# A planned attention-and-mixer kernel: a longer fixed cost for exponentials in its plan, normalisation off TensorE, and the order of its work found anew

## The chip, the cores and the metric

The kernel runs on one NeuronCore of a Trainium2 chip. The metric is the time of one execution on the device, in microseconds (us). The core's engines are TensorE (PE), which multiplies matrices into the eight banks of PSUM; VectorE (DVE); ScalarE (ACT), which here evaluates exp, tanh and gelu by its tables; GpSimd (POOL); and SyncE (SP), which here only issues DMAs. Each engine has its own list of instructions, in the order in which the kernel wrote them, and waits on semaphores for the others.

## The reference

Two layers, each an attention block and then a mixer block with an MLP, over 2048 tokens of width 448, with 16 heads of 28. The weights are the same in both layers.

```python
def _A_ref(x, wqkv, wo):                     # attention
    qkv = (x @ wqkv).reshape(B, S, 3, H, Dh).transpose(2, 0, 3, 1, 4)
    q, k, v = qkv[0], qkv[1], qkv[2]
    scores = jnp.einsum("bhqd,bhkd->bhqk", q, k) * (Dh ** -0.5)
    p = _softmax(scores, axis=-1)
    o = jnp.einsum("bhqk,bhkd->bhqd", p, v)
    return o.transpose(0, 2, 1, 3).reshape(B, S, D) @ wo

def _B_ref(x, w1, w2, w3, w4):               # mixer and MLP
    h = _gelu(_layernorm(x) @ w1)
    # four quarters of h shifted by +1, -1, +2, -2 tokens -> g0..g3
    hs = jnp.concatenate([g0, g1, g2, g3], axis=-1) @ w2
    x1 = x + hs
    return x1 + _gelu(_layernorm(x1) @ w3) @ w4

x = A_x
for _ in range(2):
    x = x + _A_ref(_layernorm(x), A_wqkv, A_wo)
    x = x + _B_ref(_layernorm(x), B_w1, B_w2, B_w3, B_w4)
```

## The kernel before

**A planner writes the order.** The kernel is a set of small tasks (Python generators, `t_exp`, `t_pv`, `k_proj`, `t_mixA` and so on) that yield operations: an engine, a planned duration, what is read and written. The class `Sched` runs all tasks at once on planned clocks, one per engine, and picks at each step the operation that can start first; between those that compete it goes by a priority. The order in which it picks is the order in which each engine's instructions are written, so planned durations have no effect on the chip except through that order. Where PE would stand idle in the plan, `keep_pe_busy` puts in fillers: groups of four matmuls of the identity with no use for the result (L2160). Constants at the top of the file steer the planner: `RANK` (priorities of tasks by layer and chunk), `Q_LEAD` (how early the query projection of a chunk starts), `R_RATE` and `D_RATE` (shares of score tiles that VectorE takes, by pair of segments), `PE_NORM`, and `XPAR` (some thresholds and modes).

**Scores and exponentials.** Per layer, the queries are cut into five chunks (three of 512 and two of 256 queries), the heads into four groups of four, the keys into blocks. A segment is one chunk, one head group and a run of keys; there are 68 segments, four to a part of the order (17 parts). PE makes score tiles of 128x512 (L1411). ScalarE takes them in units of three or two banks in turn: one exponential (L1649) reads 1536 or 1024 columns of PSUM and writes bf16 into the buffer `PT`. Its planned duration stands in `t_exp`. There are 2048 score tiles.

**The share of VectorE.** Some score tiles do not go to ScalarE but through a polynomial on VectorE, a chain of five instructions: L1493 (scaled, to integer), L1520 and L1522 (two multiply-add steps), L1524 (last step, to bf16) and L1527 (puts the exponent in), with the result in the buffer `PD` or in free slots of `vaug`. The task `t_scores` picks such tiles five to nine groups of scores ahead of where ScalarE is; when it takes one for a unit's third bank, ScalarE's exponential has two tiles instead of three.

**After the scores.** PE multiplies the exponentials with the values (`t_pv`, L820, `ps<-PT,vaug`). The sums of the softmax come out as an extra row. The task `t_norm` copies the result out (L1731, or L1733 where it adds to an earlier part) and, when the segment is the last for its queries, normalises in one of two ways, chosen by `PENORM`. One goes through DMA: the row of sums is loaded into `rT`, inverted (L1746), written to `rscr` in DRAM and spread over the partitions by four more DMAs into `fb`, and POOL multiplies (L1758). The other stays on the core: small f32 matmuls bring the sums together (`ps<-e,ub`, L820), VectorE inverts (L1771), PE and VectorE spread them out again (L1774, L1776, `ps<-rT,selq`), and VectorE multiplies (L1780). The last chunk of layer 1 always takes the second way.

```python
def PENORM(L, ch, g):
    return (L == 1 and ch == len(CHUNKS[1]) - 1) or (PE_NORM[L, ch] and g == 3)
```

**Mixer and MLP.** The output projection (`t_outproj`), the mixer (`t_mixA`, `t_mixB`) and the MLP (`t_w4`) of a chunk are done while the exponentials of later chunks go on. Their projections are the lines L829. Gelu needs another table of ScalarE than exp, and each change is a table load. `MODE` says, by chunk, how the mixer's gelu is done: by tanh, which shares the table of exp (L1929 on ScalarE, with L1927 on POOL and L1928 and L1930 on VectorE), or as one wide gelu (L1911) that waits to share a table load with the gelu of the MLP (L2113). When the last exponential is through, the tail begins: the gelus of the last groups are then read directly from PSUM (L2085), and PE works off the last projections.

Of the kernel before, what the change touches and what calls it, by code (L numbers as in the profile page):

```python
# [6 lines left out]
ACT = mybir.ActivationFunctionType  # L7
# [541 lines left out]
DPRIO = 2.5  # L549
DST = [('dve', 0.6), ('dve', 0.6), ('dve', 0.34), ('dve', 0.6)]  # L550
DSEG = 1
R_RATE = {(0,): 0.142, (1,): 0, (2,): 0.185, (3,): 0, (4,): 0, (5,): 0.02, (6,): 0.218, (7,): 0.001, (8,): 0, (9,): 0.095, (10,): 0.119, (11,): 0.363, (12,): 0.116, (13,): 0.0, (14,): 0, (15,): 0.04, (16,): 0.176, (17,): 0, (18,): 0, (19,): 0.261, (20,): 0.084, (21,): 0.12, (22,): 0.211, (23,): 0.279, (24,): 0.114, (25,): 0.159, (26,): 0.143, (27,): 0.211, (28,): 0, (29,): 0.129, (30,): 0.03, (31,): 0.098, (32,): 0.024, (33,): 0.0}
RLO = 6
RHI = 9
RPRIO = 0.5
# [3 lines left out]
DLO = 5  # L559
DHI = 8  # L560
DPK = 2
RANK = {('q', 0, 1): 1.485, ('q', 0, 2): 2.903, ('q', 0, 3): 1.285, ('q', 1, 0): 1, ('q', 1, 1): 1, ('q', 1, 2): 1.695, ('q', 1, 3): 2.124, ('b', 0, 0): 2.36, ('b', 0, 1): 1.442, ('b', 0, 2): 2.1, ('b', 0, 3): 3, ('b', 0, 4): 2.2, ('b', 1, 0): 1.217, ('b', 1, 1): 2.458, ('b', 1, 2): 2.616, ('b', 1, 3): 2.98, ('b', 1, 4): 2.111, ('a', 0, 0): 2.648, ('a', 0, 1): 2.105, ('a', 0, 2): 2.607, ('a', 0, 3): 1.825, ('a', 0, 4): 1.327, ('a', 1, 0): 1.819, ('a', 1, 1): 2.318, ('a', 1, 2): 1.312, ('a', 1, 3): 1.708, ('a', 1, 4): 2.524, ('k', 0, 1): 1.651, ('k', 0, 2): 1.127, ('k', 0, 3): 1.089, ('k', 1, 0): 2.088, ('k', 1, 1): 2.41, ('k', 1, 2): 1.843, ('k', 1, 3): 2.108, ('k', 1, 4): 1.983, ('c', 0, 0): 1.937, ('c', 0, 1): 1, ('c', 0, 2): 1.716, ('c', 0, 3): 2.026, ('c', 0, 4): 2.338, ('c', 1, 0): 2.542, ('c', 1, 1): 1.267, ('c', 1, 2): 1, ('c', 1, 3): 2.438, ('c', 1, 4): 1.368, ('w', 0, 0): 1.991, ('w', 0, 1): 1.492, ('w', 0, 2): 2.1, ('w', 0, 3): 2.652, ('w', 0, 4): 2.838, ('w', 1, 0): 2.361, ('w', 1, 1): 2.963, ('w', 1, 2): 2.611, ('w', 1, 3): 2.164, ('w', 1, 4): 1.394, ('o', 0, 0): 2.395, ('o', 0, 1): 1.387, ('o', 0, 2): 1.318, ('o', 0, 3): 1.195, ('o', 0, 4): 1.084, ('o', 1, 0): 2.093, ('o', 1, 1): 1.177, ('o', 1, 2): 1.823, ('o', 1, 3): 1.568, ('o', 1, 4): 1.308, ('v', 0, 1): 2.396, ('v', 0, 2): 1.93, ('v', 0, 3): 2.669, ('v', 1, 0): 1.95, ('v', 1, 1): 2.676, ('v', 1, 2): 2.257, ('v', 1, 3): 1.399, ('v', 1, 4): 2.602, ('l', 1, 0): 1.698, ('l', 1, 1): 2.543, ('l', 1, 2): 2.299, ('l', 1, 3): 1.01, ('l', 1, 4): 1.745}
Q_LEAD = {(0, 1): 34, (0, 2): 114, (0, 3): 36, (1, 0): 57, (1, 1): 67, (1, 2): 75, (1, 3): 147}
D_RATE = {(0,): 0.041, (1,): 0, (2,): 0, (3,): 0.154, (4,): 0.266, (5,): 0.481, (6,): 0.055, (7,): 0.125, (8,): 0.155, (9,): 0.747, (10,): 0.232, (11,): 0.243, (12,): 0.14, (13,): 0, (14,): 0.372, (15,): 0.002, (16,): 0.057, (17,): 0.442, (18,): 0, (19,): 0.418, (20,): 0.453, (21,): 0, (22,): 0.343, (23,): 0.024, (24,): 0.41, (25,): 0.544, (26,): 0.546, (27,): 0, (28,): 0.445, (29,): 0, (30,): 0, (31,): 0, (32,): 0.506, (33,): 0.438}
PE_NORM = {(0, 0): False, (0, 1): False, (0, 2): True, (0, 3): False, (0, 4): True, (0, 5): False, (0, 6): False, (0, 7): False, (1, 0): True, (1, 1): False, (1, 2): True, (1, 3): True, (1, 4): False, (1, 5): False, (1, 6): True, (1, 7): True}
TANHW = {(0, 11): 1, (1, 13): 1}
Sched.AGED = 0
Sched.TARGET = 0.6
# [33 lines left out]
def build_kernel(nc, A_x, A_wqkv, A_wo, B_x, B_w1, B_w2, B_w3, B_w4, out, n_layers=2):  # L602
# [8 lines left out]
    SCALE = DH ** -0.5  # L611
# [70 lines left out]
    with st:  # L682
# [3 lines left out]
        ps = st.enter_context(nc.psum_tensor("ps", [128, 8, 512], FP32))  # L686
# [52 lines left out]
        PT = sb("PT", [128, 15, 512], BF16)  # L739
# [522 lines left out]
        def t_kv(L, c):  # L1262
# [28 lines left out]
        def t_q(L, qc):  # L1291
# [240 lines left out]
        def t_scores():  # L1532
# [40 lines left out]
            while True:  # L1573
# [60 lines left out]
        def t_exp():  # L1634
            u = -1
            while True:
                u += 1
                yield ("wait", ("st", u))
                un = units[u]
                if not un:  # L1640
                    break
                if u >= 6:
                    for (si, kb, j) in units[u - 6]:
                        yield ("wait", ("pv", si, kb))
                bk = unit_banks(u)
# [3 lines left out]
                yield op("act", 0.051 + n * w * 0.000833, lambda e, bk=bk, s0=s0, n=n, w=w: e.activation(out=PT[:, s0:s0 + n, 0:w], in_=ps[:, bk[0]:bk[0] + n, 0:w], func=ACT.Exp, scale=SCALE),  # L1649
                         reads=[("ps", b) for b in bk], writes=[("pt", s0 + k) for k in range(n)], tab="exp")  # L1650
# [612 lines left out]
```

## Time and profile before

| | |
|---|---|
| Time, median of 3 runs | 1032.74 us (1032.65 to 1034.38) |
| Profiled execution | 1035.93 us, of which the span from first to last instruction is 1034.2 us |
| Busy: PE, DVE, ACT, POOL | 986.5, 769.1, 988.8, 280.4 us |
| Granted clock of TensorE, mean | 0.993 of full |
| Exponentials (L1649) | 352 of 128x1536, 449 of 128x1024 |
| First and last exponential start | 15.7 and 982.2 us |

A busy time counts an engine's own instructions, and overlapping ones once. The profile's busy share of PE contains the fillers. A duration of a single ScalarE instruction in the groups (a mean of 1571 ns for 128x1536) contains the time in which it overlaps with the one before it; the distance between two starts is shorter. The profiled execution is one run, some 3 us longer than the median of the timed runs.

### The profile page before, as it was taken

How to read it: one execution, taken by the hardware profiler on the slowest of the kernel's cores; microseconds unless marked ns; L12 is line 12 of the kernel's file. 1: busy time of each engine (PE TensorE's matmuls, PEld its weight loads, DVE VectorE, ACT ScalarE, POOL GpSimd, SP SyncE). 2: the span in 40 equal slices, each digit the busy share in tenths (PEclk: the TensorE clock that was granted, in tenths of full speed). 3: DMA queues.
4: the chain of work that ended last, by engine and by line, in shares of the span. 5: the costliest groups of instructions: out<-in, count | busy, mean ns of one | idle time of the engine just before them, and what ended most of it. 6: DMA issues, size and time to landing. Idle time of an engine off the chain costs nothing.

```text
span 1034.2 us, 35199 instructions
## 1 busy us (share of the span) xinstructions
PE 986.5 (95%) x15802; PEld 408.2 (39%) x15805; DVE 769.1 (74%) x1502; ACT 988.8 (96%) x907; POOL 280.4 (27%) x403
## 2 busy tenths in 40 slices
PE   8999999998999999999999999999999999899998
PEld 4333344333333344334434333333334434444465
DVE  8577887899888775667767976797886875776452
ACT  7999999999999999999999999998999999999952
POOL 2232223333205014431335021121543120422120
PEclk9999999999999999999999999998999999999999
DMA  4423645111105004111123033413201020120000
GB/s 120 133 69 87 145 118 148 40 28 36 35 12 116 13 11 111 43 43 24 46 79 63 32 88 112 140 46 107 64 23 38 18 68 2 41 71 15 12 15 31
DMA packets 97259, 63.25 MB, mean 61 GB/s; under 512 B 69908, under 2 KB 86372, under 8 KB 97108
## 3 DMA queue, kind: packets, MB, share of 16 engines
q1 hardware_dynamic: 93732, 52.91, 20.0%
q0 software_dynamic: 3376, 8.09, 3.0%
q8 instruction: 124, 2.03, 0.8%
q14 instruction: 27, 0.22, 0.1%
HBM read 27.12 MB, written 16.73 MB: 42 GB/s over the span
## 4 chain that ended last, share of the span: by engine, by line
ACT 80%; PE 15%; DVE 4%; issue 1%; DMA 0%; SPq 0%; DVEq 0%
ACT PT L1649 72%; PE ps L829 9%; PE ps L1411 3%; ACT h2T L2113 3%; PE ps L820 3%; ACT fb L1929 1%; DVE PD L1524 1%; ACT L1649 1%; ACT hT L1911 0%; PE ps L2160 0%; ACT L2113 0%; DVE fb L1520 0%; ACT L1911 0%; DVE PD L1527 0%; DMA PT<-in_A_wqkv_dram 0%
## 5 line engine op out<-in xcount | busy, mean ns | idle before, releaser
L1649 ACT ACTIVATE PT<-ps 128x1024 bf16<-128x1024 f32 (+1 forms) x801 | 893.5, 1328 | 9.9 <-PE ps L1411 9.5
L1411 PE MATMUL ps<-qT,kT 32*128 32x512 bf16 (+1 forms) x2560 | 315.4, 342 | 25.5 <-ACT PT L1649 18.5
L820 PE MATMUL ps<-PT,vaug 128*32 128x512 bf16 (+1 forms) x2452 | 247.0, 343 | 0.7 <-DVE ub L1733 0.6
L1411 PEld LDWEIGHTS ps<-qT,kT 32*128 32x128 bf16 x2560 | 80.7, 91 | 302.8 <-ACT PT L1649 284.5
L829 PE MATMUL ps<-xT,w 128*32 128x512 bf16 (+3 forms) x2368 | 158.7, 340 | 2.1 <-DVE hT L1898 1.7
L820 PEld LDWEIGHTS ps<-PT,vaug 128*32 128x32 bf16 x2452 | 74.8, 95 | 87.8 <-issue 71.9
L2160 PE MATMUL ps<-ident 128*32 128x256 bf16 x2188 | 102.2, 280 | 1.6 <-POOL ident L914 1.5
L829 PE MATMUL ps<-w,h2T 128*32 128x448 bf16 x1288 | 91.3, 355 | 4.1 <-ACT h2T L2113 4.1
L829 PEld LDWEIGHTS ps<-xT,w 128*32 128x32 bf16 x2368 | 63.5, 95 | 48.2 <-issue 22.9
L2089 DVE CAST h2T<-ps 128x384 bf16<-128x384 f32 (+1 forms) x84 | 52.1, 620 | 27.0 <-PE ps L829 26.0
L2160 PEld LDWEIGHTS ps<-ident 128*32 128x32 bf16 x2188 | 62.6, 98 | 21.8 <-issue 9.0
L1758 POOL TENSOR_TENSOR otn<-ub,fb 128x512 bf16<-128x512 f32 (+1 forms) x31 | 34.9, 1125 | 130.3 <-DMA fb<-rscr 130.2
L1493 DVE TENSOR_SCALAR yd<-ps 128x512 int32<-128x512 f32 x73 | 50.1, 687 | 25.3 <-PE ps L1411 24.4
L1163 POOL TENSOR_TENSOR sq<-qT 128x512 bf16<-128x512 bf16 x28 | 31.7, 1135 | 115.4 <-DVE qT L1212 111.8
L1163 POOL TENSOR_TENSOR sq<-kT 128x512 bf16<-128x512 bf16 (+2 forms) x32 | 31.6, 991 | 84.2 <-DVE kT L1177 68.8
L1522 DVE SCALAR_TENSOR_TENSOR fb<-fb,yd 128x512 f32<-128x512 f32 x68 | 51.2, 757 | 0.6
L1527 DVE SCALAR_TENSOR_TENSOR PD<-yd,PD 128x512 int16<-128x512 int16 x70 | 49.5, 709 | 1.0
L1520 DVE SCALAR_TENSOR_TENSOR fb<-yd 128x512 f32<-128x512 uint16 x68 | 47.1, 699 | 0.4
L829 PEld LDWEIGHTS ps<-w,h2T 128*32 128x32 bf16 x1288 | 34.3, 96 | 32.9 <-issue 14.3
L829 PE MATMUL ps<-xT,wq_pad 128*32 128x512 bf16 x512 | 43.3, 383 | 1.8 <-DVE vaug L1493 0.9
L1837 POOL TENSOR_SCALAR mst<-mv 128x1 f32<-128x1 f32 x32 | 7.8, 242 | 135.0 <-DVE mv L1016 133.5
L829 PE MATMUL ps<-xT,wk_pad 128*32 128x512 bf16 (+2 forms) x512 | 42.2, 363 | 0.3 <-DVE h2T L2089 0.2
(200 smaller groups left out, 1339.3 us busy)
## 6 DMA issues: line engine op xcount, KB each, us to landing
uscr<-ub SPq DMA_DIRECT2D x28, 256.0 KB, 2.0
ub<-uscr SPq DMA_DIRECT2D x28, 256.0 KB, 3.6
fb<-rscr SPq DMA_DIRECT2D x84, 64.0 KB, 2.1
xnd<-xn SPq DMA_DIRECT2D x28, 128.0 KB, 2.9
x_res<-in_A_x_dram POOLq DMA_DIRECT2D x16, 224.0 KB, 3.7
xd<-x_res SPq DMA_DIRECT2D x16, 224.0 KB, 2.4
x_res<-xd SPq DMA_DIRECT2D x16, 224.0 KB, 3.0
out_dram<-obf SPq DMA_DIRECT2D x16, 112.0 KB, 1.9
```

What stands on the lines that cost most here:

```text
L820: return lambda e: e.matmul(out=out, lhsT=lhsT, rhs=rhs, start=start, stop=stop, **kw)
L829: r.append(e.matmul(out=out[c:c + w, :], lhsT=lhsT[:, c:c + w], rhs=rhs, start=start, stop=stop, tile_position=(0, c)))
L1163: return both("sq", 0.15 + NW * 0.0018, 0.07 + NW * 0.00104, lambda e: e.tensor_tensor(out=sq[:, si, 0:NW], in0=src, in1=src, op=ALU.mult) ...
L1411: yield op("pe", (0.005 + NW * 0.00042) / nc_, lambda e, i=i, kc=kc, j=j, g=g, a=a, NW=NW, bank=bank: e.matmul(out=ps[:, bank, i * NW:(i + ...
L1493: yield op("dve", c_ps(512), lambda e: e.tensor_scalar(out=y, in0=ps[:, bi(bank), :], scalar1=SCALE * L2E * FS, scalar2=-126.0 * FS, op0=A ...
L1520: yield op(D_[0][0], D_[0][1], lambda e: e.scalar_tensor_tensor(out=q, in0=lo, scalar=E2 / E3 * FS, in1=lo, op0=ALU.add, op1=ALU.mult), re ...
L1522: yield op(D_[1][0], D_[1][1], lambda e: e.scalar_tensor_tensor(out=q, in0=q, scalar=E1 / E3 * FS * FS, in1=lo, op0=ALU.add, op1=ALU.mult) ...
L1527: yield op(D_[3][0], D_[3][1], lambda e: e.scalar_tensor_tensor(out=pdt.bitcast(I16), in0=hi, scalar=128.0, in1=pdt.bitcast(I16), op0=ALU. ...
L1649: yield op("act", 0.051 + n * w * 0.000833, lambda e, bk=bk, s0=s0, n=n, w=w: e.activation(out=PT[:, s0:s0 + n, 0:w], in_=ps[:, bk[0]:bk[0 ...
L1758: yield both("otn", 0.2 + NW * 0.0021, 0.07 + NW * 0.00104, lambda e: e.tensor_tensor(out=otn[:, g, 0:NW], in0=u, in1=rb[:, 0:NW], op=ALU. ...
L2089: ev = op("dve", c_ps(m * NW), lambda e, hr=hr, pv=pv: e.tensor_copy(out=hr, in_=pv), reads=[("ps", bi(b))], writes=hk, touch=[b])
L2160: return [e.matmul(out=ps[32 * c:32 * c + 32, bi(b), 0:256].rearrange("p (a n) -> p a n", n=128), lhsT=xn[:, 0, D:D + 32] if live else ide ...
```

## The change

The planned duration of an exponential has 0.0635 instead of 0.051 as its fixed part. The constants of the planner are replaced: `RANK`, `Q_LEAD`, `R_RATE`, `D_RATE`, some of `XPAR`, and `PE_NORM`, which is now false for every chunk but the last one of layer 1 (entries for chunks 5 to 7 have no chunk). In `XPAR`, the entry of the mixer of layer 0, chunk 1 goes from 1 to 0, that is from the wide gelu to tanh; the other entries `mg` that differ choose nothing, since chunk 0 and the last chunk of layer 1 are decided otherwise. All the rest is the planner's answer to these numbers.

```diff
...
-R_RATE = {(0,): 0.142, (1,): 0, (2,): 0.185, (3,): 0, (4,): 0, (5,): 0.02, (6,): 0.218, (7,): 0.001, (8,): 0, (9,): 0.095, (10,): 0.119, (11,): 0.363, (12,): 0.116, (13,): 0.0, (14,): 0, (15,): 0.04, (16,): 0.176, (17,): 0, (18,): 0, (19,): 0.261, (20,): 0.084, (21,): 0.12, (22,): 0.211, (23,): 0.279, (24,): 0.114, (25,): 0.159, (26,): 0.143, (27,): 0.211, (28,): 0, (29,): 0.129, (30,): 0.03, (31,): 0.098, (32,): 0.024, (33,): 0.0}
+R_RATE = {(0,): 0, (1,): 0.172, (2,): 0.006, (3,): 0.003, (4,): 0.021, (5,): 0, (6,): 0.317, (7,): 0, (8,): 0.118, (9,): 0.112, (10,): 0.118, (11,): 0.453, (12,): 0.316, (13,): 0, (14,): 0, (15,): 0.344, (16,): 0.26, (17,): 0, (18,): 0, (19,): 0.017, (20,): 0.197, (21,): 0.08, (22,): 0, (23,): 0.396, (24,): 0.016, (25,): 0, (26,): 0.013, (27,): 0.22, (28,): 0, (29,): 0.17, (30,): 0.146, (31,): 0.157, (32,): 0.079, (33,): 0.151}
...
-Q_LEAD = {(0, 1): 34, (0, 2): 114, (0, 3): 36, (1, 0): 57, (1, 1): 67, (1, 2): 75, (1, 3): 147}
-D_RATE = {(0,): 0.041, (1,): 0, (2,): 0, (3,): 0.154, (4,): 0.266, (5,): 0.481, (6,): 0.055, (7,): 0.125, (8,): 0.155, (9,): 0.747, (10,): 0.232, (11,): 0.243, (12,): 0.14, (13,): 0, (14,): 0.372, (15,): 0.002, (16,): 0.057, (17,): 0.442, (18,): 0, (19,): 0.418, (20,): 0.453, (21,): 0, (22,): 0.343, (23,): 0.024, (24,): 0.41, (25,): 0.544, (26,): 0.546, (27,): 0, (28,): 0.445, (29,): 0, (30,): 0, (31,): 0, (32,): 0.506, (33,): 0.438}
-PE_NORM = {(0, 0): False, (0, 1): False, (0, 2): True, (0, 3): False, (0, 4): True, (0, 5): False, (0, 6): False, (0, 7): False, (1, 0): True, (1, 1): False, (1, 2): True, (1, 3): True, (1, 4): False, (1, 5): False, (1, 6): True, (1, 7): True}
+Q_LEAD = {(0, 1): 36, (0, 2): 36, (0, 3): 26, (1, 0): 25, (1, 1): 89, (1, 2): 73, (1, 3): 71}
+D_RATE = {(0,): 0.191, (1,): 0.073, (2,): 0.708, (3,): 0, (4,): 0.398, (5,): 0, (6,): 0.055, (7,): 0.125, (8,): 0.181, (9,): 0.094, (10,): 0.687, (11,): 0.099, (12,): 0, (13,): 0.327, (14,): 0.127, (15,): 0.488, (16,): 0.002, (17,): 0.163, (18,): 0.072, (19,): 0, (20,): 0.146, (21,): 0, (22,): 0.064, (23,): 0.07, (24,): 0.388, (25,): 0.814, (26,): 0.353, (27,): 0, (28,): 0.257, (29,): 0, (30,): 0.439, (31,): 0.207, (32,): 0.452, (33,): 0.089}
+PE_NORM = {(0, 0): False, (0, 1): False, (0, 2): False, (0, 3): False, (0, 4): False, (0, 5): False, (0, 6): False, (0, 7): False, (1, 0): False, (1, 1): False, (1, 2): False, (1, 3): False, (1, 4): True, (1, 5): False, (1, 6): True, (1, 7): False}
...
-XPAR = {'l0': 7, 'l1': 12, 'l2': 15, 'x0': 14, ('mg', 0, 0): 1, ('mg', 0, 1): 1, ('mg', 0, 2): 0, ('mg', 0, 3): 1, ('mg', 0, 4): 1, ('mg', 1, 0): 0, ('mg', 1, 1): 1, ('mg', 1, 2): 0, ('mg', 1, 3): 0, ('mg', 1, 4): 1, 'rp': 0.807, 'dp': 2.739, 'dt': 0.642, 'ft': 0.068}
+XPAR = {'l0': 10, 'l1': 9, 'l2': 15, 'x0': 14, ('mg', 0, 0): 0, ('mg', 0, 1): 0, ('mg', 0, 2): 0, ('mg', 0, 3): 1, ('mg', 0, 4): 1, ('mg', 1, 0): 1, ('mg', 1, 1): 1, ('mg', 1, 2): 0, ('mg', 1, 3): 0, ('mg', 1, 4): 0, 'rp': 0.531, 'dp': 2.743, 'dt': 0.642, 'ft': 0.068}
...
-                yield op("act", 0.051 + n * w * 0.000833, lambda e, bk=bk, s0=s0, n=n, w=w: e.activation(out=PT[:, s0:s0 + n, 0:w], in_=ps[:, bk[0]:bk[0] + n, 0:w], func=ACT.Exp, scale=SCALE),
+                yield op("act", 0.0635 + n * w * 0.000833, lambda e, bk=bk, s0=s0, n=n, w=w: e.activation(out=PT[:, s0:s0 + n, 0:w], in_=ps[:, bk[0]:bk[0] + n, 0:w], func=ACT.Exp, scale=SCALE),
...
```

The two built programs differ in these counts:

| | before | after |
|---|---|---|
| Exponentials of three and of two tiles (L1649) | 352 and 449 | 348 and 448 |
| Score tiles on VectorE (L1493) | 94 | 108 |
| Normalisations on TensorE (L1780), by DMA (L1758) | 9 and 31 | 4 and 36 |
| Tanh of 112x512 (L1929) | 16 | 20 |
| Gelus of 112x2048 (L1911) | 2 | 1 |
| Table loads on ScalarE | 14 | 14 |
| Filler matmuls (L2160) | 2964 | 3676 |

More of the change, by code (lines that the diff above doesn't have):

```diff
@@ L565 @@
-PE_NORM = {(0, 0): False, (0, 1): False, (0, 2): True, (0, 3): False, (0, 4): True, (0, 5): False, (0, 6): False, (0, 7): False, (1, 0): True, (1, 1): False, (1, 2): True, (1, 3): True, (1, 4): False, (1, 5): False, (1, 6): True, (1, 7): True}
+RANK = {('q', 0, 1): 1, ('q', 0, 2): 2.926, ('q', 0, 3): 1.344, ('q', 1, 0): 1.16, ('q', 1, 1): 1.448, ('q', 1, 2): 2.482, ('q', 1, 3): 2.694, ('b', 0, 0): 2.69, ('b', 0, 1): 3, ('b', 0, 2): 2.117, ('b', 0, 3): 3, ('b', 0, 4): 1.3, ('b', 1, 0): 1.54, ('b', 1, 1): 2.659, ('b', 1, 2): 2.395, ('b', 1, 3): 2.656, ('b', 1, 4): 1.785, ('a', 0, 0): 2.682, ('a', 0, 1): 2.137, ('a', 0, 2): 2.193, ('a', 0, 3): 1.528, ('a', 0, 4): 2.177, ('a', 1, 0): 2.554, ('a', 1, 1): 1.339, ('a', 1, 2): 2.144, ('a', 1, 3): 1.716, ('a', 1, 4): 1.378, ('k', 0, 1): 1.671, ('k', 0, 2): 1.153, ('k', 0, 3): 2.3, ('k', 1, 0): 1.509, ('k', 1, 1): 1.159, ('k', 1, 2): 2.29, ('k', 1, 3): 2.008, ('k', 1, 4): 2.047, ('c', 0, 0): 2.322, ('c', 0, 1): 1, ('c', 0, 2): 2.312, ('c', 0, 3): 2.29, ('c', 0, 4): 2.895, ('c', 1, 0): 1.835, ('c', 1, 1): 2.728, ('c', 1, 2): 1, ('c', 1, 3): 1.063, ('c', 1, 4): 2.113, ('w', 0, 0): 2.585, ('w', 0, 1): 1.381, ('w', 0, 2): 2.188, ('w', 0, 3): 2.222, ('w', 0, 4): 1.577, ('w', 1, 0): 2.097, ('w', 1, 1): 2.531, ('w', 1, 2): 2.441, ('w', 1, 3): 1.365, ('w', 1, 4): 2.19, ('o', 0, 0): 2.109, ('o', 0, 1): 2.018, ('o', 0, 2): 1.228, ('o', 0, 3): 1, ('o', 0, 4): 2.301, ('o', 1, 0): 2.412, ('o', 1, 1): 1.252, ('o', 1, 2): 2.047, ('o', 1, 3): 1.075, ('o', 1, 4): 1.098, ('v', 0, 1): 1.913, ('v', 0, 2): 2.642, ('v', 0, 3): 1.559, ('v', 1, 0): 2.058, ('v', 1, 1): 1.264, ('v', 1, 2): 1, ('v', 1, 3): 1.537, ('v', 1, 4): 2.768, ('l', 1, 0): 1.265, ('l', 1, 1): 1.774, ('l', 1, 2): 2.73, ('l', 1, 3): 2.089, ('l', 1, 4): 2.648}
```

1 line of the change is left out of this document (removed).

## The prediction

> **What bounds the kernel now.** The page comes first: busy times, then the chain that ended last.
>
> ```profile
> PE 986.5 (95%) x15802; PEld 408.2 (39%) x15805; DVE 769.1 (74%) x1502; ACT 988.8 (96%) x907; POOL 280.4 (27%) x403
> ACT 80%; PE 15%; DVE 4%; issue 1%; DMA 0%; SPq 0%; DVEq 0%
> ```
>
> ScalarE (ACT) carries 80% of the chain, and nearly all of that is the exponentials of line 1649. PE looks as busy, but much of it is filler (L2160), and the next view, the waits, shows who waits for whom.
>
> ```profile
> PEld ps L1411 <- ACT PT L1649: 284.5, 728, 1.4
> ACT PT L1649 <- PE ps L1411: 9.5, 12, 1.9
> ```
>
> The weight loads of the score matmuls wait 728 times for an exponential to free its banks; the exponentials wait 12 times. So ACT sets the pace from 16 to 984 us, and a tail led by PE follows. The chain in order of time gives the price of an exponential, alone and in a long run:
>
> ```profile
> 585.61 1.34 ACT PT L1649
> 587.46 0.92 ACT PT L1649
> 826.07 63.10 ACT PT L1649 x58
> ```
>
> The 1.34 is one of three score tiles, the 0.92 one of two: a tile costs some 0.427 us (starts in the timeline lie 1.331 and 0.904 apart). The run of 58 holds 35 of two and 23 of three, 139 tiles: 63.10 - 139 x 0.427 = 3.75, or 0.065 per exponential for the fixed part with its small slips, although the unbroken pair leaves 0.904 - 0.854 = 0.05. The plan's new 0.0635 is the mean of a run, the old 0.051 the floor.
>
> The stretches, last, show where ACT is not full (columns: length, busy time of PE, weight loads, DVE, ACT, POOL, then PE's granted clock, DMA share, GB/s):
>
> ```profile
> 699.20:716.20 17.00, 16.24 (x139) 6.53 (x143) 11.59 (x23) 13.99 (x13) 2.88 (x2) 0.70 0.49 134
> ...
> 931.00:936.00 5.00, 5.00 (x64) 1.75 (x64) 3.50 (x7) 4.09 (x4) 0.00 (x0) 0.66 0.02 5
> ...
> 665.50:697.90 32.40, 30.29 (x482) 12.10 (x470) 29.44 (x52) 32.40 (x31) 5.38 (x5) 1.00 0.26 69
> 697.90:736.40 38.50, 36.85 (x412) 13.50 (x410) 29.25 (x55) 35.48 (x32) 13.52 (x19) 0.87 0.37 100
> ...
> 983.50:1034.20 50.70, 47.47 (x1086) 29.79 (x1084) 19.39 (x39) 19.92 (x28) 7.69 (x16) 0.99 0.07 23
> ```
>
> ACT idles 17.00 - 13.99 = 3.0 and 5.00 - 4.09 = 0.9 us where PE's clock was cut. Just before stand TensorE normalisations:
>
> ```profile
> 702.74 0.61 PE L820 MATMUL ps<-e,ub 128*128 128x4 f32 x4
> ...
> 926.31 0.61 PE L820 MATMUL ps<-e,ub 128*128 128x4 f32 x4
> ```
>
> The other three that the change removes (368, 492 and 864 us) left the clock full. Ahead of 700, DVE was busy 29.44 of 32.40 us, and the chain runs through it from 691 to 700: a late DVE began that stall.
>
> **The change, part by part.** The new order is read from the two built programs; prices are rows of before.
>
> *Exponentials.* Score tiles on ACT fall from 1954 to 1940: 352 to 348 exponentials of three, 449 to 448 of two. Saved: 4 x 1.34 + 0.92 = 6.3 us, all on the path, as ACT idles in few places. The longer fixed part in the plan is no instruction; it costs nothing itself and acts only through the order.
>
> *One gelu session less shared.* In layer 0 the mixer of chunk 1 goes from a gelu of 112x2048 (1.91) to four tanh of 112x512 (1.04 a pair in the chain): +0.2. Table loads stay at 14. DVE gets eight instructions more (0.84 and 0.70, 6 us) and POOL four (1.28); they lie beside ACT, priced under DVE.
>
> *Five normalisations off TensorE.* Gone on PE are 40 small f32 matmuls of that form and on DVE some 6 us; instead each issues six DMAs on SP (2.1 us to landing), a reciprocal (0.33) and a POOL product (1.31 or 0.73). The longer way, two DMAs in turn and the four broadcasts after them, delays that chunk's output projection by some 5 us. Scores of the next chunk, 55 to 120 us of exponentials, cover it; uncovered, it would be 5 us once. The DMAs queue on SP with loads for later chunks, and POOL is busy 27%. What it may bring is the clock: 3.0 + 0.9 us at most, nothing at least. I take -3.0, since two of the five fall right before the run's only two cuts, yet DVE had part in the first.
> The Trainium skill, page "TensorE: Matmul & The Clock Gate", Part 1, ties the half clock to a PE idle window of about 3.4 us. PE was busy 16.24 of 17.00 us, so the rows do not agree with it; by that rule the removal brings nothing and the sum is 3 us higher.
>
> *Fourteen more DVE chains (94 to 108).* A chain is L1493, L1520, L1522, L1524, L1527: 0.69 + 0.70 + 0.76 + 0.49 + 0.71 = 3.3 us as recorded, some 2.7 at the 0.60 step that the chain shows. With the tanh steps and less the normalisations, each instruction at its line's busy mean, DVE rises from 769 to 811 us. On the whole this lies beside ACT; by stage it does not everywhere. In the parts of the order that ran from 637 to 698 us, DVE work was 51.8 us against 60.5 of ACT; it becomes 60.8 against 59.6. From 858 to the last exponential it goes from 84 against 119 to 101 against 117. What the chains make is used five to nine groups of scores later, so a lag of some us is borne. Least: nothing, below nothing excluded as DVE only gains work. Most: three stalls like the 3.0 us after 697.9, +9. I take half such a stall, +1.5, nearest to the one stretch with DVE above ACT.
>
> *Fillers.* L2160 goes from 2964 to 3676 matmuls, 178 groups of four at some 0.11 us (24 took 0.84), 20 us of PE. They stand where PE waits anyway (the 284.5 us) and help the clock: nothing. Without that cover each delays a score by 0.11.
>
> *Head.* Two chains now stand in the first part (its DVE work goes from 38.1 to 44.7 us) where the chain of before runs through DVE more than once. Between 0 and one 2.0 us gap; I take +0.5.
>
> *Tail.* After the last score matmul PE now has 32 up-projection matmuls of 512 columns (4 before) and 224 of 256 (204). At 0.0414 per 384 columns (224 took 9.28), that is 28 x 0.055 + 20 x 0.03 = +2.1; before's tail has 50.70 - 47.47 = 3.2 us of idle PE to take some. ACT gets two gelus from PSUM (0.59 each) and 1024 columns less in the last wide one (0.9): +0.3. Between -0.5 and +2.4; I take +1.0.
>
> *Sum.* -6.3 + 0.2 - 3.0 + 1.5 + 0.5 + 1.0 = -6.1. The profiled execution took 1035.93 (span 1034.2 and 1.7 around it), so it becomes 1029.8; the median lies 3.2 below the profiled one, hence 1026.6.
>
> **Rivals.**
>
> *DVE becomes the bound (slower).* Score tiles shifted to DVE pay only while DVE keeps up; from the point where its queue lags by more than the five to nine groups, PV matmuls and with them buffers and scores wait. For: the stretch with 60.8 against 59.6, and the stall of before that began at 29.44 of 32.40. Against: DVE at 44.73 of 50.00 us (200 to 250) cost ACT only 0.8. Three stalls of 3.0 in the later parts with more DVE work (637 to 698 and 736 to 984 us), the clock cuts not regained, head and tail as above: -6.1 - 1.5 + 9 + 3.0 = +4.4, or 1037. Chance 0.28.
>
> *The clock cuts stay (or others come).* They came from the late DVE and not from the normalisation, as three of five passed without. Then -6.1 + 3.0 = -3.1: 1029.6. Chance 0.17.
> The Trainium skill's page "TensorE: Matmul & The Clock Gate", Part 1, gives normalisations no part in a cut either.
>
> *Gain given back.* ACT does 6 us less, but an order paced 796 x 0.0125 = 10 us slower than ACT's floor makes ACT wait in small pieces. For: PE and DVE are placed by plan times. Against: a run's mean is 0.065, so the plan comes nearer to the chip. Some 6 us lost: 1032.7. Chance 0.10.
>
> *The change does not do what it says:* excluded; the built order shows 4 products of line 1780 instead of 9 and the 14 chains.
>
> **How the numbers follow.** Forecast 0.45, DVE-bound 0.28, clock 0.17, given back 0.10. A measurement of this kernel can tell some 0.2%, or 2.1 us, from no change, so faster means under 1030.7. That is the forecast and most of the clock case, 0.45 + 0.13 = 0.58; same is 0.10 + 0.04 = 0.14; slower 0.28. The low end takes the best of each term: -6.1 - 3.9 - 0.5 = -10.5, and 1 us of smaller gaps: 1021 after rounding down. The high end reaches to the middle of the DVE case, 1037, which leaves about 0.14 above it and little below the low end.
>
> **What would show it.** Right: 1940 tiles in 796 exponentials, ACT busy some 6 us lower; clock 1.00 through the stretches that answer to 699 to 716 and 931 to 936; DVE near 811; span of the exponentials shorter by 7 to 8 us, tail longer by about 1. Wrong: waits of L1649 for L1411 well above 9.5 us, with DVE instructions in the chain where scores or PV matmuls wait for L1527, L1212 or L1241; a new cut of the clock; or a tail longer by over 3 us.

## The result, and the profile after

| | before | after |
|---|---|---|
| Time, median of the runs | 1032.70 us (1032.65 to 1034.38, 4 runs) | 1041.04 us (1039.78 to 1042.08, 4 runs) |
| Profiled execution, span | 1035.93, 1034.2 us | 1041.67, 1039.8 us |
| Score tiles on ScalarE | 1954 | 1940 |
| Last exponential starts at | 982.2 us | 985.2 us |

The changed kernel is slower: ratio 1.0076, 95% interval 1.0061 to 1.0091. ScalarE has 6 us less to do, and yet its last exponential starts 3 us later (8 us later than in e1 below, where the kernel before ran without the clock cuts of its profiled execution).

The page of the profile after, busy times and chain:

```profile
PE 987.6 (95%) x16437; PEld 418.2 (40%) x16437; DVE 813.0 (78%) x1565; ACT 985.6 (95%) x907; POOL 296.7 (29%) x412
ACT 63%; PE 26%; DVE 9%; DMA 1%; issue 1%; SPq 0%; POOL 0%; DVEq 0%
```

ACT's share of the chain falls from 80 to 63%, DVE's rises from 4 to 9%. The waits say the same (who waited for whom: us in total, times, longest):

```profile
PEld ps L1411 <- ACT PT L1649: 252.4, 667, 1.4
...
ACT PT L1649 <- PE ps L1411: 15.1, 16, 3.2
```

The exponentials now wait 15.1 us for scores, where they waited 9.5. The chain in order of time (start, length, what) shows three places that the text below returns to:

```profile
86.40 10.16 DMA xT<-xnd
...
141.60 1.80 DVE fb L1522
...
164.45 1.68 DVE fb L1520
...
176.88 1.69 DVE fb L1520
...
994.18 3.02 PE ps L829 x60
997.75 14.28 PE ps L829 x335
1013.57 23.27 PE ps L829 x528
```

A transposed load is in the chain for 10 us; steps of the polynomial are recorded with 1.7 to 1.8 us, not 0.69; and the last stretch of PE is 23.27 us long, where before had `1010.88 20.42 PE ps L829 x460`.

Two stretches of the windows view (length, then busy time of PE, weight loads, DVE, ACT, POOL, granted clock, DMA share, GB/s) answer to those of before. The first is the only place with a cut clock, the second the tail:

```profile
96.00:100.00 4.00, 3.40 (x26) 0.80 (x26) 0.14 (x1) 1.02 (x1) 0.00 (x0) 0.57 0.02 8
...
986.40:1039.80 53.40, 49.95 (x1160) 33.54 (x1160) 18.62 (x39) 20.18 (x31) 7.79 (x16) 1.00 0.07 22
```

**Where the time is.** ScalarE's list up to the last exponential can be split in every trace into work (0.051 us and 0.000833 per column for each activation, 1.283 for a table load, all from distances between starts) and the rest, its gaps; with the tail from the start of the last exponential the three make the span. "Before again" is experiment e1, an execution of the kernel before in which the clock was full throughout. "Both undone" is experiment e9: the changed kernel with the two costs taken away that the experiments find, one of them by shortened products on POOL. "Before, short products" is experiment e7, the kernel before with the same shortening, so e9 has to be compared with e7; both ran at full clock.

| us | before again (e1) | before, short products (e7) | after | both undone (e9) |
|---|---|---|---|---|
| Work of ScalarE to the last exponential | 949.3 | 949.3 | 943.3 | 943.3 |
| Gaps up to 51 us | 10.6 | 10.6 | 12.1 | 12.1 |
| Gaps from there on | 16.5 | 14.3 | 29.1 | 17.7 |
| Tail | 52.0 | 52.0 | 54.5 | 54.5 |

The columns add up, with the first 0.8 us and within 0.1, to the spans of 1029.3, 1027.0, 1039.8 and 1028.4. From e1 to after, before rounding: -6.1 + 1.5 + 12.5 + 2.5 is +10.5. The 12.5 is the question.

### The profile page after: what moved, and what is told of

It is laid out like the page before. It is cut to its first block, busy times and chain, and to the rows that moved or that the text cites. A ratio compares the mean times of both kernels' runs of the same rounds, so it can differ in the third digit from the quotient of the medians.

```text
span 1039.8 us, 36565 instructions
## 1 busy us (share of the span) xinstructions
PE 987.6 (95%) x16437; PEld 418.2 (40%) x16437; DVE 813.0 (78%) x1565; ACT 985.6 (95%) x907; POOL 296.7 (29%) x412
## 4 chain that ended last, share of the span: by engine, by line
ACT 63%; PE 26%; DVE 9%; DMA 1%; issue 1%; SPq 0%; POOL 0%; DVEq 0%
ACT PT L1649 56%; PE ps L829 13%; PE ps L1411 6%; PE ps L820 4%; ACT h2T L2113 3%; PE ps L2160 2%; DVE fb L1520 1%; ACT fb L1929 1%; DVE PD L1527 1%; DVE fb L1522 1%; DMA xT<-xnd 1%; DVE PD L1524 1%; DVE yd L1493 1%; ACT L1649 1%; ACT L2113 0%
## 5 line engine op out<-in xcount | busy, mean ns | idle before, releaser
L1649 ACT ACTIVATE PT<-ps 128x1024 bf16<-128x1024 f32 (+1 forms) x796 | 889.7, 1286 | 16.1 <-PE ps L1411 15.1
L829 PE MATMUL ps<-xT,w 128*32 128x512 bf16 (+4 forms) x2592 | 178.2, 344 | 2.3 <-DVE hT L1898 1.8
L2160 PE MATMUL ps<-ident 128*32 128x256 bf16 x2772 | 123.3, 277 | 3.2 <-POOL ident L914 1.5
L1758 POOL TENSOR_TENSOR otn<-ub,fb 128x512 bf16<-128x512 f32 (+1 forms) x36 | 44.0, 1223 | 171.6 <-DMA fb<-rscr 165.0
L829 PE MATMUL ps<-w,h2T 128*32 128x448 bf16 x1288 | 88.6, 355 | 3.4 <-ACT h2T L2113 3.4
L829 PEld LDWEIGHTS ps<-xT,w 128*32 128x32 bf16 (+1 forms) x2592 | 70.2, 95 | 53.1 <-issue 24.2
L2160 PEld LDWEIGHTS ps<-ident 128*32 128x32 bf16 x2772 | 77.0, 97 | 28.0 <-issue 11.2
L1493 DVE TENSOR_SCALAR yd<-ps 128x512 int32<-128x512 f32 x83 | 56.8, 687 | 20.5 <-PE ps L1411 20.1
L1527 DVE SCALAR_TENSOR_TENSOR PD<-yd,PD 128x512 int16<-128x512 int16 x79 | 57.6, 730 | 0.9
L1163 POOL TENSOR_TENSOR sq<-kT 128x512 bf16<-128x512 bf16 (+2 forms) x32 | 32.7, 1030 | 84.4 <-DVE kT L1177 71.1
L1520 DVE SCALAR_TENSOR_TENSOR fb<-yd 128x512 f32<-128x512 uint16 x76 | 56.4, 751 | 0.3
L1522 DVE SCALAR_TENSOR_TENSOR fb<-fb,yd 128x512 f32<-128x512 f32 x76 | 55.6, 736 | 0.5
L1927 POOL TENSOR_TENSOR fb<-hT 112x512 f32<-112x512 bf16 (+1 forms) x28 | 32.0, 1142 | 60.4 <-DVE hT L1898 25.0
L829 PEld LDWEIGHTS ps<-w,h2T 128*32 128x32 bf16 x1288 | 35.6, 96 | 31.8 <-issue 12.8
L829 PE MATMUL ps<-xT,wk_pad 128*32 128x512 bf16 (+1 forms) x512 | 42.9, 369 | 2.1 <-DVE x1b L1998 0.9
L829 PE MATMUL ps<-wv,xT 128*32 128x448 bf16 x480 | 38.9, 363 | 3.4 <-DMA xT<-xnd 2.9
```

The lines of the kernel that those rows point to most:

```text
L829: r.append(e.matmul(out=out[c:c + w, :], lhsT=lhsT[:, c:c + w], rhs=rhs, start=start, stop=stop, tile_position=(0, c)))
L1163: return both("sq", 0.15 + NW * 0.0018, 0.07 + NW * 0.00104, lambda e: e.tensor_tensor(out=sq[:, si, 0:NW], in0=src, in1=src, op=ALU.mult) ...
L1493: yield op("dve", c_ps(512), lambda e: e.tensor_scalar(out=y, in0=ps[:, bi(bank), :], scalar1=SCALE * L2E * FS, scalar2=-126.0 * FS, op0=A ...
L1520: yield op(D_[0][0], D_[0][1], lambda e: e.scalar_tensor_tensor(out=q, in0=lo, scalar=E2 / E3 * FS, in1=lo, op0=ALU.add, op1=ALU.mult), re ...
L1522: yield op(D_[1][0], D_[1][1], lambda e: e.scalar_tensor_tensor(out=q, in0=q, scalar=E1 / E3 * FS * FS, in1=lo, op0=ALU.add, op1=ALU.mult) ...
L1527: yield op(D_[3][0], D_[3][1], lambda e: e.scalar_tensor_tensor(out=pdt.bitcast(I16), in0=hi, scalar=128.0, in1=pdt.bitcast(I16), op0=ALU. ...
```

## Experiments

Unless a diff says otherwise, the order of all instructions is kept, so that one cause changes alone. Times are medians, ratios are to the kernel before measured on the same chip.

**e1: the kernel before once more**, unchanged.

> The kernel before, unchanged, profiled once more. Theory of the prediction (normalisations on TensorE bring the clock down): the clock cuts near 705 and 931 us come again, with about 3 us of idle ScalarE time at each run. Rival (the first cut was an accident of the one profiled execution, which at 1035.9 us lay 3.2 above the median): no cut of 10 us near 705, profiled time within 1 us of 1032.7.

Measured: 1030.98, one execution, 1.7 below the median of before and not within 1 us of it, since that median contains cuts too (see below). Its windows, between the same exponentials as the two stretches in which the profiled execution of before had granted clocks of 0.70 and 0.66:

```profile
699.14:712.26 13.12, 11.97 (x139) 5.13 (x135) 10.69 (x20) 13.12 (x13) 3.01 (x3) 1.00 0.54 138
927.30:931.10 3.80, 3.80 (x72) 1.57 (x73) 3.39 (x7) 3.80 (x5) 0.00 (x0) 1.00 0.02 6
```

Same instructions, clock 1.00, ACT busy all the time, and 13.1 us instead of 17.0 for the first stretch. So the cuts do not come with every execution of the program. Over all 72 executions of before in these experiments, the 21 with a mean clock of 1.000 have a median of 1031.5 us, the 30 with 0.998 one of 1032.6, the 11 with 0.997 one of 1033.9. In the traces a cut is to 0.5 and lasts a multiple of 3.41 us, unless the run ends in it: 10.24 us from 705.7 and 3.41 from 930.98 in before, 3.41 from 96.45 in after, 6.83 in e2 and in e5. A mean of 0.998 is thus one short cut, 3.41 x 0.5 of 1030 us.

**e2 and e6: the weight loads.** On POOL the changed order has the memset of `wo_pad` and seven weight loads (lines 870 to 875) earlier in its list. The plan put them near 93 us, behind an exponential, but that wait exists only in the plan, and POOL issued them at 82 to 87 us (before: 102 to 107). They collide with the transposed load of line 1148. Rows of the timeline, after (start, length, engine, line, instruction, then idle time before it):

```profile
82.27 2.66 POOL L870 DMA_DIRECT2D wo_pad<-in_A_wo_dram  x4 [0.31 <-POOL wo_pad L1006]
...
86.40 6.37 SPq L1148 DMA_TRANSPOSE xT<-xnd  x1
...
96.61 0.94 PE L829 MATMUL ps<-wv,xT 128*32 128x448 bf16 x8 [2.91 <-DMA xT<-xnd]
...
98.12 1.02 ACT L1649 ACTIVATE PT<-ps 128x1024 bf16<-128x1024 f32 x1 [2.84 <-PE ps L1411]
```

The load, issued at 86.40, lands at 96.56; PE stands still 2.9 us in front of the value projection, the clock is cut, and the exponentials wait. In the 10.16 us between, the DMA engines were full (windows of after):

```profile
86.40:96.56 10.16, 7.29 (x109) 2.76 (x106) 4.18 (x7) 8.82 (x9) 0.68 (x1) 0.99 1.00 230
```

In before the same load was issued at 86.37; its transposed loads of this line took 4.3 to 6.5 us to landing.

e2 moves the loads to a later place in POOL's list; e6 lets them wait on the chip for the exponential (number 62) that the plan had:

```diff
 # e2
+        anchor = [o for o in P.ops["pool"] if o.dma and o.fn.__code__.co_firstlineno == 1792][0]
+        ... (lines 870, 873, 874, 875 put ahead of anchor)
 # e6
+        after = [o for o in exps if o.pos > max(x.pos for x in set_)][0]
+        ... (the same loads put behind it in the order)
+        moved[0].deps["act"] = after
```

> The order of the changed kernel on every engine, but POOL issues the seven weight loads of wo, w1 and w2 only ahead of its first loads of the residual (after 104 us, where the kernel before had them) instead of at 82 to 87 us. Theory: these loads make the transposed load of 86.4 us land after 10.2 us instead of some 5, and PE's value projection waits for it; then the wait and the clock cut after it go, ScalarE's gaps at 94 and 98 us (4.2 us) go, and the time falls by 3 to 4 us from 1041.0 to about 1037.3. Rival (the lag is taken up by waits for VectorE soon after, which now end later): under 1 us.

> The order of the changed kernel on all engines; the seven weight loads of wo, w1 and w2 wait on the chip for exponential 62 (about 94 us), where the plan put them, instead of running at 82 to 87 us as soon as POOL is free. Theory: the transposed load of 86.4 us lands in some 5 us instead of 10, the gaps at 94 and 98 us (4.2 us) and the clock cut go: 1041.0 to about 1037. In the run with the loads moved to 107 us the same gap had moved to the next transposed load (111 us). Rival (the transposed load is slow for another reason): under 1 us.

e2 took 1045.78 (1042.12 to 1049.61; ratio 1.0130, 1.0109 to 1.0151), a miss by 8 us. The loads, now issued at 107 to 112, met the next transposed load:

```profile
112.47 5.73 SPq L1148 DMA_TRANSPOSE xT<-xnd  x1
116.38 2.37 ACT L1649 ACTIVATE PT<-ps 128x1536 bf16<-128x1536 f32 x2 [4.23 <-PE ps L1411]
120.10 2.37 ACT L1649 ACTIVATE PT<-ps 128x1536 bf16<-128x1536 f32 x2 [1.36 <-PE ps L1411]
```

The cure was not right; that the cause was, e6 shows. It took 1037.61 (1036.68 to 1039.01; ratio 1.0052, 1.0037 to 1.0067): 3.4 less than after, as expected. The two intervals of the ratios still touch, but the traces are clear: ScalarE's gaps at 98 and 100 us, 4.2 us together, are gone, and all its gaps behind 51 us fall from 29.1 to 24.4, by 4.7. Its loads go out from 95.9 us, between two transposed loads, and no instruction waits for one.

**e3 and e4: a lighter chain.** The steps L1522 and L1527 work on 64 of 512 columns, in the changed kernel and in the kernel before; those score tiles are not the reference's.

```diff
-    yield op(D_[1][0], D_[1][1], lambda e: e.scalar_tensor_tensor(out=q, in0=q, ..., in1=lo, ...),
+    yield op(D_[1][0], D_[1][1], lambda e: e.scalar_tensor_tensor(out=q[:, 0:64], in0=q[:, 0:64], ..., in1=lo[:, 0:64], ...),
...
```

> The order of the changed kernel, but in each of the 108 chains the two in-place steps (the second multiply-add and the exponent step) work on 64 of 512 columns, so the score tiles that go through VectorE are not computed fully. This takes about 0.5 us from each of 216 instructions, some 105 us of VectorE work, with no instruction moved. Theory (a late VectorE takes the gain): the gaps of ScalarE at 144, 168, 181, 190, 335 to 344, 720, 769 and 784 us go, about 8 us, and part of the head's: 1041.0 to about 1032.5. Rival (the plan's slower pace makes ScalarE wait for PE): under 2 us.

> The same cut in the chains of the kernel before (94 chains, same order as before). Theory: it loses less to a late VectorE, so it gains less: 3 to 5 us, to about 1028.5; the difference of the two light kernels is then what head, weight loads and tail make, 4 to 7 us, less the 6 us of exponentials. Rival (VectorE cost both the same): it gains as much as the changed kernel does, and the 8 us between them stay.

After: 1030.72 (ratio 0.9986, 0.9977 to 0.9995), 10.3 less. Before: 1029.53 (ratio 0.9971, 0.9960 to 0.9982), 3.2 less. So a late VectorE costs the kernel before some 3 us and the changed one some 10; about 3 of these are the wait at 94 us, which shrank here too (with the loads still early, the transposed load took 8.45 us).

**e5 and e7: the products on POOL.** A DVE instruction with two operands in SBUF, while POOL multiplies in f32 (rows of the timeline, after):

```profile
140.88 0.68 DVE L1520 SCALAR_TENSOR_TENSOR fb<-yd 128x512 f32<-128x512 uint16 x1
141.58 1.27 POOL L1758 TENSOR_TENSOR otn<-ub,fb 128x512 bf16<-128x512 f32 x1 [26.06 <-DMA fb<-rscr]
141.60 1.79 DVE L1522 SCALAR_TENSOR_TENSOR fb<-fb,yd 128x512 f32<-128x512 f32 x1
```

The product ends at 142.85, and the DVE step 0.54 later, so most of its usual 0.69 lies behind the product, as if it had begun to work only when POOL was through. The Trainium skill, page "SBUF — State Buffer", section "SBUF: two separate sides", says why: a DVE instruction with two SBUF inputs and a POOL instruction that reads SBUF need the same pair of ports, and whichever starts first holds it for its whole length. The rows agree. e5 (after) and e7 (before) shorten the product to 64 columns; the rest of the normalised output is set to zero once, next to the memset of `wo_pad`:

```diff
-  ... e.tensor_tensor(out=otn[:, g, 0:NW], in0=u, in1=rb[:, 0:NW], op=ALU.mult),
+  ... e.tensor_tensor(out=otn[:, g, 0:64], in0=u[:, 0:64], in1=rb[:, 0:64], op=ALU.mult),
-  yield op("pool", 2.0, lambda e: e.memset(wo_pad[:, :, :], 0.0), writes=[("woz",)])
+  yield op("pool", 2.0, lambda e: [e.memset(otn[:, :, :], 0.0), e.memset(wo_pad[:, :, :], 0.0)], writes=[("woz",)])
```

> The order of the changed kernel; POOL's 36 normalisation products (L1758) work on 64 of 512 columns, so the normalised heads of the other columns are left out (POOL clears that buffer once at 80 us). Theory: while POOL does such a product (1.27 us and more), a VectorE instruction next to it takes 1.4 to 1.8 us instead of 0.6, and these push VectorE over the edge: the gaps of ScalarE that follow products (144, 168, 181, 190, 335 to 338, 769, 784 us, together some 6.5 us) go, 1041.0 to about 1034.5. Rival (VectorE is late by the amount of chain work alone): under 2 us.

> The same short products in the kernel before (31 of them, order as before). Theory: it has only two gaps of some 0.9 us that follow a product (219 and 749 us), so it gains 1 to 2 us: about 1031. Rival (products cost both kernels alike): as much as the changed kernel gains.

The same place in e5:

```profile
144.81 0.69 DVE L1522 SCALAR_TENSOR_TENSOR fb<-fb,yd 128x512 f32<-128x512 f32 x1
144.94 0.74 POOL L1758 TENSOR_TENSOR otn<-ub,fb 128x64 bf16<-128x64 f32 x1 [26.21 <-DMA fb<-rscr]
```

DVE's step is back at 0.69, and the stalls of ACT near 144, 168, 190, 769 and 784 us are gone; near 335 us one of 0.97 is left. But e5 took 1038.25 (ratio 1.0060, 1.0043 to 1.0077), 2.8 less and not 6.5. What was missing is at 94 us, and the experiment's own edit made it: the added memset put the weight loads 1.8 us later on POOL, from 84.05 us, so that they lay right over the transposed load, whose landing took still longer:

```profile
86.45 12.12 DMA xT<-xnd
```

e7 took 1031.95 (ratio 0.9991, 0.9978 to 1.0005), by its median not to be told from before. But eight of its ten executions had cut clocks (0.992 to 0.998). The two at 1.000 took 1028.7, where before at 1.000 takes 1031.5. The trace of e7 is one of these two, and there the gaps of 0.9 us at 219 and 749 us are gone, as the theory had it; the gaps behind 51 us are 14.3 us against 16.5 in e1. The waits of the exponentials, in e1 and then in e7:

```profile
ACT PT L1649 <- PE ps L1411: 5.6, 6, 1.9
```

```profile
ACT PT L1649 <- PE ps L1411: 4.2, 4, 1.9
```

So the kernel before, too, pays some 2 us for its products; the median hides it behind clock cuts. Why e7 has so many of them is open.

**e9: loads held and products shortened**, the edits of e6 and e5 in one kernel.

> The changed kernel, its order kept, with two of the suspected costs taken away at once: the weight loads of GpSimd wait for the exponential behind which the plan had them, and the GpSimd products of line 1758 work on 64 of their 512 columns (the rest of the normalised output stays zero). If the two causes are separate, their effects add: 1041.0 less 3.4 for the loads and about 6 for the products (of which the product experiment alone showed 2.8, since the wait at 94 us grew by some 3), so 1031 to 1032. If the products' effect was only 2.8 and the growth of the wait at 94 us had nothing to do with it: 1041.0 - 3.4 - 2.8 = 1034.8. If the wait only moves on to another place: 1037 or more.

1030.22 (1029.93 to 1033.53; ratio 0.9976, 0.9965 to 0.9988): 10.8 less than after. Behind the held loads the products are worth 1037.61 - 1030.22 = 7.4. The waits of the exponentials:

```profile
ACT PT L1649 <- PE ps L1411: 6.1, 4, 3.2
```

From 15.1 us in 16 waits to 6.1 in 4, of which 3.2 is the one in the head. The gaps behind 51 us fall by 11.4 us, 4.7 with the loads (e6) and 6.7 with the products, so the two effects add up. But 2.2 for products are in the kernel before as well (e7). Of the 12.5 us that the change added, the loads therefore make about 4.7, the products 4.5, and 3.4 are left, the difference of e9 and e7 (17.7 and 14.3). What is left is in small pieces: ScalarE's gaps of 0.02 to 0.3 us sum to 10.0 us in e7 and 14.0 in e9. The two kernels with a light chain show the same, 9.6 in e4 and 13.0 in e3. Most of the growth is where PE does a projection (L829) right ahead of the scores that an exponential waits for: 6.4 us in 74 gaps in e7, 9.4 in 105 in e9. No run takes these pieces away, so their cause stays open.

**e14: the head.** The same as e9, and the two chains that now stand ahead of exponential 25 made light, as in e3.

> The changed kernel as in the run before with both undone (1030.2), and in the two polynomial chains that stand ahead of exponential 25 the steps L1522 and L1527 on 64 of 512 columns (those two score tiles come out wrong). That takes some 2 us off VectorE ahead of the queries of the second chunk. If these chains make the gap near 46 us longer: the gap falls from 3.5 to about 2.2 and the time to 1028.9. If the gap comes from TensorE's or the transposes' order there: unchanged at 1030.2.

1030.42 (ratio 0.9985, 0.9975 to 0.9996): nothing. The exponential behind the gap in the head, in before and then in e14 (timeline):

```profile
50.76 2.37 ACT L1649 ACTIVATE PT<-ps 128x1024 bf16<-128x1024 f32 x2 [1.88 <-PE ps L1411]
```

```profile
50.88 2.37 ACT L1649 ACTIVATE PT<-ps 128x1536 bf16<-128x1536 f32 x2 [3.20 <-PE ps L1411]
```

It starts at the same time in both, 50.8 to 50.9 us, since it needs the queries of the second chunk. The changed kernel has one exponential of three tiles fewer ahead of it (24 with 60 tiles; before 25 with 63), so ScalarE is done 1.3 us sooner and waits 1.3 us longer. The longer gap is no delay; it is a part of the saving that can't be had there.

**e13 and e15: the tail.** Both start from e9. e13 leaves out up-projection matmuls behind the last scores, e15 half of the last 112 matmuls; hidden values and outputs are then incomplete.

```diff
 # e13
+        gone = up[512][-4:] + up[256][-13:]      # operations of four matmuls each
+        P.ops["pe"] = [o for o in pe if o not in gone]
 # e15: the same with 14 operations of w4 and h2T behind the last up-projection
```

> The changed kernel as in the run before with both undone (1030.2), and behind the last scores 16 up-projection matmuls of 512 columns and 52 of 256 left out of TensorE's list (inner steps of their sums over the model width, so those hidden values are incomplete). By 0.055 and 0.029 that is 0.9 + 1.5 = 2.4 us of TensorE work, about what the tail has grown by. If TensorE sets the tail: 1030.2 - 2.4 = 1027.8, the time behind the last exponential near 52. If the gelus, GpSimd or the output DMAs set it: 1030, unchanged.

> The changed kernel with both undone (1030.2), and at the very end 56 of the 112 last matmuls (w4 from h2T, inner steps, so those outputs are incomplete) left out: 56 x 0.0489 = 2.7 us of TensorE behind the last transposes, the part that the kernel before did ahead of them. If the order of this work sets the longer tail: 1030.2 - 2.7 = 1027.5 and a last stretch of TensorE of 20.5 instead of 23.3. If the output DMAs or VectorE end the run: less than 1 us gained.

e13: 1030.12, unchanged (the tail is 54.2 instead of 54.5). With 2.4 us of matmuls gone its chain runs through POOL, and PE stops in front of the last chunk's projection:

```profile
996.81 2.45 POOL x_res L2013 x2
1002.44 22.66 PE ps L829 x508
```

POOL's two additions of line 2013 stand ahead of the rsqrt for the last normalisation, and so ahead of the transposes. So this work is not what makes the tail longer. e15: 1028.49 (ratio 0.9954, 0.9928 to 0.9979), 1.7 less, the span 1.9; the other 0.8 of the 2.7 went into a wait for a gelu and its neighbours (`1020.96 2.67 PE ps L829 x52` starts 0.5 us late behind ACT). Before does 56 of these matmuls while it waits for the last transposes; the changed order does up-projections there and leaves all 112 for the end, where nothing hides them.

**e8, e10, e11, e12: one part of the change alone.** Here the planner orders everything anew: the constants of after with the old `PE_NORM` (e8) or the old fixed part (e12), and those of before with the new fixed part (e10) or the new `PE_NORM` (e11).

```diff
 # e8: after with before's PE_NORM          # e11: before with after's PE_NORM
 # e12, on after
-  yield op("act", 0.0635 + n * w * 0.000833, ...
+  yield op("act", 0.051 + n * w * 0.000833, ...
 # e10, on before: the reverse
```

> The changed kernel's constants with the entries of the kernel before for normalisation on TensorE (five of them on again), planned anew. Theory (five more products on POOL and the longer way make VectorE late): 3 to 6 us faster than the changed kernel, 1035 to 1038. Rival (what counts is the rest of the order): within 2 us of 1041, or worse.

> The kernel before with the longer fixed part of the exponential in its plan as the only edit; the planner then orders everything anew with the constants of before. 1958 score tiles on ScalarE instead of 1954 (352 exponentials of three and 451 of two). If the plan's fixed part matters by itself because the plan comes nearer to the chip: two exponentials of two cost 1.8, and smaller gaps give back up to 6, so 1028 to 1034. If the constants fit only the plan they were found with, as the last replanned kernel showed: 1040 or more, with stalls of several us at places where before has none.

> The kernel before with the normalisations off TensorE (the entries of the change) as the only edit; the order is the same up to the first of them, near 360 us, and planned anew behind it. 99 score tiles on VectorE instead of 94, 353 exponentials of three and 445 of two, so 1.34 - 4 x 0.92 = -2.3 us of ScalarE. If taking the normalisations off TensorE costs nothing by itself: 1030 to 1033. If the DMA way's delay and the extra products on GpSimd cost: 1035 to 1040. If any planning anew with constants found for another order loses: 1040 or more, with large stalls.

> The changed kernel with the old fixed part of the exponential in its plan as the only edit; all other constants are those of the change, and the order is planned anew. 1947 score tiles on ScalarE instead of 1940, so 0.9 x 2 + 1.34 = 3.2 us more of exponentials, and 101 chains on VectorE instead of 108. If fewer chains relieve VectorE and the fixed part has no effect of its own: about 1041. If the longer fixed part is what makes this order fit: 1045 or more.

| | median | ratio, 95% interval |
|---|---|---|
| e8 | 1082.48 | 1.0489, 1.0467 to 1.0511 |
| e10 | 1047.44 | 1.0137, 1.0110 to 1.0163 |
| e11 | 1049.98 | 1.0164, 1.0149 to 1.0179 |
| e12 | 1050.86 | 1.0184, 1.0151 to 1.0217 |

All four are slower than both kernels, e8 by 41 us against after, where 3 to 6 less had been expected. It has one wait of 21.3 us that neither parent has (waits of e8):

```profile
ACT PT L1649 <- PE ps L1411: 44.1, 25, 21.3
```

A single constant moves the whole order, and `RANK`, `Q_LEAD` and the shares were found for another one. These runs therefore don't say what the normalisation or the fixed part is worth. That holds for e12 too, where the time expected for "the longer fixed part is what makes this order fit", 1045 or more, came true: e10, which has the longer fixed part, and e11, which doesn't touch it, lost more.

## Why the prediction was wrong, point by point

**Exponentials: right.** 1940 tiles in 796 exponentials; ScalarE's work to the last of them fell by 6.1 us, as the sum had it (-6.3 + 0.2).

**The clock, -3.0: wrong, and the step was one of bookkeeping.** The prediction took the gain against the profiled execution (1035.93) and then subtracted the 3.2 us by which that lies above the median. But the cuts at 705 and 931 us were why that execution lay above the median (e1: without them 1030.98). So most of the 3 us were counted twice: the median of before contains about 1 us of cuts (1032.6 with one short cut, 1031.5 with none). Whether the normalisations of TensorE have a part in the cuts is open. In e1 they ran at full clock, with the same list of DVE work in front of them, so neither they nor the late DVE, which the rival "the clock cuts stay" named, brings a cut about by itself. But in the changed order without the wait at 94 us (e6, e9, e13, e14, e15) 29 of 39 executions had a mean clock of 1.000, against 21 of 72 of before, so something in the changed order goes with fewer cuts, worth about 1 us in the median. No run with the order kept takes the normalisations alone away.
The only cut in the trace of after, from 96.45 us, comes at the end of PE's wait of 2.9 us for the transposed load. The rule of the Trainium skill's page "TensorE: Matmul & The Clock Gate", Part 1, fits that better than the cuts of before: an idle PE goes ahead of it, if one of 2.9 and not 3.4 us. In the profiled execution of before PE was idle for at most 0.9 us at a time in the 90 us ahead of its cuts at 705 and 931 us.

**The DVE term, +1.5: a late DVE was foreseen, but not what makes it late.** The weighed stretches after 637 us were not where it happened; most stalls came at 144 to 190 and at 335 us, five after 719. The prediction added up DVE's busy time by stage, at the durations of before, and set the norm edit at nothing on DVE because POOL was busy 27% only. The edit puts 36 products on POOL instead of 31, and 14 more chains beside them. The DVE instructions that ran beside POOL lost 22.7 us in all in e1 and 31.3 in after, 13.9 of it to the products of line 1758 (e1: 11.4). Each is counted by its length over the median of its form without POOL beside it, where over 0.25 us, and put down to the POOL instruction that it overlapped longest. The two sums for the products are not far apart; what they do to ScalarE is, 6.7 us of gaps in after (e6 to e9) and 2.2 in before (e1 to e7). Where a chain is late already, one such step of 1.8 us is a stall. So the change's share is 4.5 us by the gaps, against the 1.5 taken and within the bound of 9.

**The loads of the weights: not in the sum at all.** In the built order POOL's loads stand earlier, and the prediction did not ask what they pass. They cost 3.4 us by the medians and 4.7 by the gaps (e6), and more when they lie right over the transposed load (e5).

**Head, +0.5, and tail, +1.0:** they measured +1.5, within its bound of 2.0, and +2.5, just above its bound of 2.4. In the head the reason was another (e14). In the tail the sum had the matmuls right by kind of work, +2.1 of up-projections, but priced the wrong ones: those that precede the last transposes are covered by POOL (e13), those that come after are not (e15).

**Fillers at nothing: right** as far as seen. The exponentials of e9, which has all 3676 of them, wait 6.1 us in all, and its small gaps right behind a filler sum to 1.9 us, against 1.4 in e7 with 2964.

**The rivals.** "DVE becomes the bound" had the sign and a part of the mechanism: DVE was late, but by its collisions with POOL as much as by its own work (taking either away, e9 or e3, ends most of the stalls), and earlier in the run than the later parts that it named. Its 1037 was 4 short, about the weight loads' 3.4, which is luck, as its three stalls are not those that came. "Gain given back" had a mechanism that is there: ScalarE does wait in small pieces in the new order, 3.4 us more than in the old one (e9 against e7), where the rival took 6 and the sum nothing. That the plan's slower pace is the reason is not shown.

So the forecast was too low by 3.0 for the clock, 3.0 for the products (4.5 for 1.5), 4.7 for the loads, 3.4 for the small pieces, 1.0 for the head and 1.5 for the tail, together 16.6 us. These are read against e1 at full clock, 1.7 us below the median of before; 16.6 - 1.7 = 14.9 answers to the 14.4 us between the forecast and 1041.0.

With both causes away the changed order took 1030.22 against 1032.98 of before on the same chip, 2.8 us less. That is not what the order is worth: before has cut clocks more often, and e9 has short products where before has full ones. Like for like, in the full-clock traces of e9 and e7, the changed order is 1.4 us slower (1028.4 and 1027.0): about -6.1 of work, +1.5 in the head, +3.4 in gaps and +2.5 in the tail. No variant with the reference's full work was faster than the kernel before.

## What to carry to other kernels

A median and a profile are two different executions: before a gain is read from a stall in the profile, see whether the median contains that stall. Two kernels are compared at the same granted clock and with the same cost taken out of both; otherwise a cost that both pay is put down to the change, and small waits that only one has are overlooked. An engine that is busy 27% is not free if it shares something with one that is busy 75%: price the collision of two instructions, not the sums of their busy times. And of any instruction that a new order moves, transfers first of all, ask what holds it in place on the chip; a wait that exists only in the plan holds nothing.

## What the runs showed of the hardware

A DVE step of 0.69 us took 1.79 when a POOL product of 1.27 began 0.02 us ahead of it, and 0.69 when the product had 64 columns and began after it.

A transposed load, 4.3 to 7.2 us from issue to landing in two executions of before, took 10.2 us beside the weight loads (3.6 MB, issued within 5 us; the DMA engines were full), and 12.1 when they overlapped it more. The Trainium skill, page "DMA: Bandwidth & Descriptors", section "Queues, rings and completion order", says that each DMA engine serves its queues in turn, packet by packet. That fits the longer landing, but no run here separates it from other explanations; in after the issue on SP was longer too, 6.37 us instead of 2.19 in before, though not in e5 (2.50).

The granted clock of one and the same program differs from one execution to the next (mean 0.99 to 1.000 in before), and 0.002 of it goes with 1.1 us. The cuts are to 0.5, in multiples of 3.41 us. They came behind a wait of PE (2.9 us in after, 4.4 in e2, 4.9 in e5), and also without one (before).
